# Block attention and two MLPs on one core: two groups of half-array matmuls per pair of heads, later weight sums, stores by half

## Chip, core and metric

The kernel runs on one NeuronCore of a Trainium2 chip. The metric is the time of one execution on the device in microseconds (us), and before and after are compared by the median of several runs. The core's engines are TensorE (PE, matrix products into the PSUM memory, eight banks of 512 fp32 columns), VectorE (DVE), ScalarE (ACT), GpSimd (POOL) and SyncE (SP, which here only issues DMAs). Each engine works through its own queue in order and waits on semaphores for the others.

## What is computed

Four batches of eight heads, 576 positions, head width 64, go through attention with a mask by blocks of 64; its output `x` (2304 tokens, 512 wide) goes through a gated MLP (inner width 1536) and then through an MLP with a leaky ReLU (inner width 2048):

```python
scores = scale * np.matmul(q, k.transpose(0, 1, 3, 2))
scores = np.where(block_i >= block_j, scores, -1000000000.0)
attn = np.exp(scores - np.max(scores, axis=-1, keepdims=True))
attn = attn / (np.sum(attn, axis=-1, keepdims=True) + 1e-09)
x = np.matmul(attn, v)                       # then heads side by side: 2304 x 512
x = (1 / (1 + np.exp(-(x @ w_gate))) * (x @ w_val)) @ w_out
h = x @ w_in
out = np.maximum(0.01 * h, h) @ w_out        # of the second MLP
```

## The kernel before, in words

The whole program is written as a list of operations (`Plan.op`), each with an engine (or a choice of two), a cost in us that the author wrote down, what it reads and writes, the ring buffers it uses, and a due time. `Plan.order` then puts them in one order per engine: among the operations that its own clock holds ready it takes the one with the earliest due time. Nothing of that clock is left in the program; what stays is the order on each queue. A ring (`Ring`) hands out its buffers strictly in the order in which the code asked for them, so an operation that needs buffer number n waits until number n minus the ring's size is free.

The stages are these. First the attention of batch 0 alone. Then stage 0: both MLPs of batch 0 on PE, with the attention of batch 1 in between. Stage 1: both MLPs of batch 1, with the attention of batches 2 and 3 in between. Then the MLPs of batches 2 and 3 together (`pair_unit`), in a form of matrix product that needs seven instead of eight block products and for that wants sums of weight blocks.

**Attention** (`attention`, from line 339) goes by pairs of heads, since a head is 64 wide and two heads fill 128 rows. A pair has four query tiles of 128 positions (0 to 3) and a rest of 64 positions of each head ("last"). For a set of tiles `query_tiles` asks for PSUM banks, makes the score products (`scores`, line 357, which use half of the array's rows for each head), then `softmax` on DVE (line 398: mask, minimum and copy out of PSUM), ACT (line 413: exponential), DVE (lines 423 and 426: sum plus epsilon, reciprocal) and ACT or POOL (lines 431, 433: scaling), and then transposes on PE (line 544) whose results are copied back to SBUF. The products with the values (`p_v` line 568, `last_p_v` line 505) use half of the array's columns. The products of halves are gathered by `stretch`: whatever stands in the list `later` is put in front of the next score products, so that they follow each other directly on PE. In batches 1 to 3 a pair has three such stretches: (A) the value products of the pair before, the scores of "last" and of tiles 0 and 1; (B) the value products of "last" and the scores of tile 2; (C) the scores of tile 3. Between them run the matrix products of the MLPs (line 996, 12 matmuls to a unit of 256 or 320 columns). PSUM is split into rings: `mm` three banks, `sc` two, `tp` two, `pa` one. Transposes and the products for "last" use `tp`, score tiles use `sc`.

**Weights.** Each of the 68 weight tiles arrives in a packed form, is converted once (`convert`: load into a `raw` buffer, ACT lines 682 and 685, DVE lines 686 to 693, DVE or POOL line 699, then a high part on ACT or DVE and a low part on DVE into a `w` buffer) and stored; later uses load the stored form (`w<-wd`). The last four to be converted, those of batch 0's last output group (`o`), come after the first four gates of batch 1 in the code. `sums` (line 733) adds weight blocks of two neighbouring tiles for the last stage: it takes two `wf` buffers and three `raw` buffers, and its stores are `ds<-raw`. Rings: `raw` three, `wf` three, `w` seven. In the main loop at the end `sums` is called as soon as the second half of an odd tile of batch 1 has been placed, thus twice ahead of those last four conversions.

**Outputs** are stored by SP (line 296, `out_t<-acc`) in pieces of 128 x 576 once both halves of a tile are complete; the halves are 256 and 320 columns.

Of the kernel before, what the change touches and what calls it, by code (L numbers as in the profile page):

```python
# [202 lines left out]
def block_attention_then_two_mlps(  # L203
# [74 lines left out]
    def c_dve(n):  # L278
        return 0.07 + n / 960
# [57 lines left out]
    def attention(b, start, length, alone):  # L337
# [31 lines left out]
        def stretch(parts, t):  # L369

            parts = [*(make(t) for make in later), *parts]
            later.clear()

            def f():
                for x in parts:
                    x[1]()

            reads, writes, uses = [[y for x in parts for y in x[k]] for k in (2, 3, 4)]
            op("pe", sum(x[0] for x in parts), f, reads, writes, uses, t, kind="h", slack=slack)
            for x in parts:  # L380
                for then in x[5:]:
                    then()

        def softmax(tiles, masked, t):


            nm, sm, r = r_nm.tile(), r_sm.tile(), r_r.tile()
            done, k = [], 0
            m = len(tiles)
            for i, pieces in enumerate(tiles):  # L390
                x = tiles_made[0] % NPP
                tiles_made[0] += 1
# [24 lines left out]
                op(  # L417
                    "act", c_act(n) + 0.14, f, [(nm, k - 1), *[(p_tok, j) for j in range(len(pieces))]],
                    [(sm, i), p_tok], [nm, sm, both], t + 1.3,
                )  # L420
                done.append((pt, p_tok, n))

            op("dve", 0.07, lambda: nc.vector.tensor_scalar(
                out=r[:, :m], in0=sm[:, :m], scalar1=1e-9, scalar2=None, op0=ALU.add
            ), [(sm, i) for i in range(m)], [r], [r, sm], t + 2.2)
            op("dve", 0.08, lambda: nc.vector.reciprocal(out=r[:, :m], in_=r[:, :m]), [], [r], [r], t + 2.4)  # L426
            for i, (pt, p_tok, n) in enumerate(done):

                def f(e, pt=pt, i=i, n=n):
                    if e == "act":  # L430
                        nc.scalar.activation(pt[:, :n], pt[:, :n], AF.Copy, scale=r[:, i:i + 1])  # L431
                    else:
                        nc.gpsimd.tensor_scalar(  # L433
                            out=pt[:, :n], in0=pt[:, :n], scalar1=r[:, i:i + 1], scalar2=0.0, op0=ALU.mult, op1=ALU.add
                        )

                op(("act", "pool"), (0.24 + n / 1200, 0.25 + n / 1200), f, [r], [p_tok], [r, both], t + 2.6, port=("pool",))
            return [x[:2] for x in done]

        def pair(i):  # L440
# [30 lines left out]
                return r  # L471


            beside = []

            def last_queries(t):

# [34 lines left out]
                        lambda: split(S - BLK, S, "D", t + 0.8, px, [px]),  # L512
                    )

                later.append(last_p_v)
                if alone:
                    stretch([], t + 5.2)

            def query_tiles(cs):
                t = at[cs[0]]  # L520
                ps = [bank(), bank()]
                cols = dict(zip(cs, (0, P)))
                if cs[0] == 0 and not alone:
                    beside.extend([(b_tp.tile(), 0, 4 * P), (ps[0], 3 * P, BLK)])
                scores(
                    of_last(beside if cs[0] == 0 else [])
                    + [(ps[a], cols[c], 0, a, c * P, P, 0, (c + 1) * P) for c in cs for a in range(2)], tqk, t,
                )
                done = softmax([[(ps[a], cols[c], (c + 1) * P)] for c in cs for a in range(2)], True, t)
                for c in cs:  # L530
                    transposed(c, done[2 * cs.index(c):][:2], at[c])

# [49 lines left out]
                if alone:  # L582
                    stretch([], t + 5.2)

            for cs in ([0, 1], [2], [3]):
                query_tiles(cs)
                if cs[0] == 0 and not alone:
                    last_queries(at[0])
            if alone:
                last_queries(at[NKT - 1])  # L590

        for i in range(H // 2):
            pair(i)
# [76 lines left out]
    def convert(u, wf, d):  # L670
# [27 lines left out]
        def f(e):  # L698
            engines[e].tensor_tensor(wf[:].bitcast(I32), mag[:].bitcast(I32), rnd[:], ALU.add)  # L699

        op(("dve", "pool"), (c_dve(n) + 0.03, 1.23), f, [mag, rnd], [wf], [mag, rnd, wf], d - 5, port=True)

    seen = set()

# [18 lines left out]
    def sums(u, w0, w1):  # L723
# [5 lines left out]

        def two(n, out, x, y, alu, reads, writes, uses, d):  # L730
            op(
                both_engines, (c_dve(n), 0.2 + n / 490),
                lambda e: engines[e].tensor_tensor(out(), x(), y(), alu), reads, writes, uses, d, port=True,
            )

# [90 lines left out]
    def mix_tile(first, e, half, k):  # L826
# [3 lines left out]

        def two(out, x, y, alu, reads, writes, uses, e):
            op(
                ("dve", "pool"), (c_dve(n), 0.2 + n / 490),
                lambda eng: engines[eng].tensor_tensor(out[:, hs], x(), y(), alu), reads, writes, uses, e, port=True,
            )

# [42 lines left out]
    def pair_unit(u, ws, half):  # L879
# [56 lines left out]
        def finish(name, p, x):  # L936
# [10 lines left out]
            else:  # L947
                view, gtok, ghost = gates[b, m + j]
                op(
                    ("dve", "pool"), (c_dve(n), 0.2 + n / 490),  # L950
                    lambda e: engines[e].tensor_tensor(dst(), dst(), view()[:, hs], ALU.mult),
                    [(gtok, half)], [tok], [host, ghost], e, port=True,
                )
# [21 lines left out]
    def half_unit(u, ws, half):  # L975
# [66 lines left out]
        else:  # L1042
# [7 lines left out]
            if kind == "y" and g == N1 // G - 1 and b < 2:  # L1050
                toks = x_toks(b, mo, "CD" if half else "A")
                hi_lo(n, lambda: x_of(b, mo)[:, 0, hs], lambda: x_of(b, mo)[:, 1, hs], lambda: a, toks_a, *toks, [], e + 0.6)
            if kind == "o" and g == N2 // G - 1 and half:
                store(
                    out[mo * P:(mo + 1) * P, b * S:(b + 1) * S], lambda: acc_of(b)[:, mo], P * S * 4, e + 1,
                    [*toks_of(b, mo, 0), *toks_of(b, mo, 1)], [("out", b, mo)],
                )


    attention(0, 5.0, FIRST, True)  # L1060
    held, sl = {}, []
    sums_x = None

    def g_place(t, view, i=0, more=()):
# [16 lines left out]
    for n, (u, half) in enumerate(order):  # L1081
# [31 lines left out]
            held[key] = weights(u)  # L1113
        half_unit(u, held[key], half)
        if u[1] == 1 and u[0] in ("gate", "val", "h") and u[2] % 2 and half:
            sums(u, held[u[0], 1, u[2] - 1], held[u])

    with tc.manual_schedule():
        make_identity(nc, ident)
# [53 lines left out]
```

## Time and profile before

| | |
|---|---|
| median of 3 runs (lowest to highest) | 1033.25 us (1030.99 to 1036.31) |
| the profiled execution: its time | 1031.44 us |
| its span, first to last instruction | 1029.7 us |
| PE busy | 1009.4 us, 98% of the span |
| DVE / ACT / POOL busy | 716.1 / 529.9 / 161.8 us |
| DMA | 200 MB, 194 GB/s on average |
| transposes and "last" products on PE, lines 544, 490, 505 | 400 matmuls of 128 columns and 320 of 64 |

The span is what the trace shows; the profiled execution's time is 1.74 us longer, the parts before the first and after the last recorded instruction. In the rows further down, a row of the timeline gives the start and the length of a run of like instructions in us; the end of a matmul is modelled, so the distance from the start of one row to the start of the next is the safer measure on PE. In each stretch of a window table an engine's busy time can be set against the length of the stretch. `sc<-qk ... 64x384 x4` are the scores of tile 2 for two heads; every product of plain fp32 stands in the trace as two matmuls.

### The profile page before, as it was taken

Reading aid. Unit: us, or ns where it says so; the run is one execution under the profiler, and the core shown is the slowest. Engines: PE = TensorE matmul, PEld = TensorE weight load, DVE = VectorE, ACT = ScalarE, POOL = GpSimd, SP = SyncE. Lnnn points to the kernel's source line nnn. Section 1 sums busy time; section 2 is a strip of 40 time slices with the busy share of each in tenths; the row PEclk is TensorE's granted clock in tenths of the full one; section 3 lists DMA queues with packets and bytes.
Section 4 is the critical chain, followed back from the end, with each engine's and each line's share of the span. In section 5 each row is a group of like instructions: output and inputs, shape, how many; then the busy total and the mean of one; then the engine's idle time right before and its main releaser. Section 6 shows DMA issues by size and latency. Waiting matters only on the chain.

```text
span 1029.7 us, 20204 instructions
## 1 busy us (share of the span) xinstructions
PE 1009.4 (98%) x7680; PEld 937.9 (91%) x7680; DVE 716.1 (70%) x1773; ACT 529.9 (51%) x1178; POOL 161.8 (16%) x186
## 2 busy tenths in 40 slices
PE   7999999999998999999999999999999999999998
PEld 4588998999996998889889889999999999999998
DVE  6989899999976876467656458860844887163652
ACT  7987776888748365545654543242321444231220
POOL 3321112211111413124122202100200110000000
PEclk9999999999999999999999999999999999999999
DMA  9686867688876797665765445452442435242422
GB/s 221 186 302 224 303 234 254 237 291 276 287 268 220 293 311 256 200 208 183 237 205 191 138 154 190 152 189 99 146 164 68 149 114 184 72 164 67 162 80 92
DMA packets 69985, 200.03 MB, mean 194 GB/s; under 512 B 6912, under 2 KB 16128, under 8 KB 69888
## 3 DMA queue, kind: packets, MB, share of 16 engines
q1 hardware_dynamic: 69888, 198.73, 58.4%
q8 instruction: 61, 1.00, 0.4%
q14 instruction: 36, 0.29, 0.1%
HBM read 137.36 MB, written 61.34 MB: 193 GB/s over the span
## 4 chain that ended last, share of the span: by engine, by line
PE 91%; ACT 3%; DVE 2%; DMA 2%; issue 1%; SPq 0%; POOL 0%; POOLq 0%; DVEq 0%; ACTq 0%
PE mm L996 55%; PE mm L899 6%; PE tp L899 6%; PE sc L899 6%; PE sc L357 4%; PE tp L544 3%; PE pa L899 3%; PE pa L568 2%; DMA raw<-in_w 1%; PE tp L357 1%; PE mm L568 1%; DMA w<-wd 1%; PE tp L490 1%; PE tp L505 1%; ACT both L413 1%
## 5 line engine op out<-in xcount | busy, mean ns | idle before, releaser
L996 PE MATMUL mm<-g,w 128*128 128x256 f32 (+1 forms) x1776 | 272.3, 299 | 0.9 <-DVE w L303 0.7
L996 PE MATMUL mm<-x,w 128*128 128x256 f32 (+1 forms) x1920 | 270.6, 298 | 2.2 <-DVE gf L1023 1.4
L996 PEld LDWEIGHTS mm<-x,w 128*128 128x128 f32 x1920 | 256.6, 188 | 13.2 <-issue 5.2
L996 PEld LDWEIGHTS mm<-g,w 128*128 128x128 f32 x1776 | 247.3, 190 | 10.4 <-issue 3.5
L1049 DVE TENSOR_TENSOR acc<-mm,acc 128x256 f32<-128x256 f32 (+1 forms) x160 | 72.8, 455 | 87.6 <-PE mm L996 86.9
L413 ACT ACTIVATE both<-both,nm 128x128 f32<-128x128 f32 (+3 forms) x144 | 82.9, 578 | 31.7 <-DVE nm L398 31.1
L899 PE MATMUL sc<-x,w 128*128 128x256 f32 (+1 forms) x480 | 76.3, 295 | 1.0 <-ACT v L301 1.0
L699 POOL TENSOR_TENSOR wf<-mag,rnd 128x512 int32<-128x512 int32 x34 | 46.6, 1372 | 192.9 <-DVE mag L693 130.7
L398 DVE CUSTOM_DVE_ANT_0 both<-sc,mask 128x128 f32<-128x128 f32 (+4 forms) x121 | 53.7, 483 | 27.7 <-PE sc L357 27.2
L314 DVE TENSOR_TENSOR g<-gf,g 128x576 fp32r<-128x576 f32 (+2 forms) x92 | 62.5, 685 | 13.7 <-ACT g L301 13.5
L996 PE MATMUL mm<-sg,w 128*128 128x320 f32 (+1 forms) x416 | 70.2, 294 | 0.0
L899 PEld LDWEIGHTS sc<-x,w 128*128 128x128 f32 x480 | 67.8, 188 | 1.2 <-ACT v L301 1.2
L996 PE MATMUL mm<-qk,w 128*128 128x320 f32 (+1 forms) x384 | 66.8, 296 | 0.0
L301 ACT ACTIVATE g<-gf 128x576 fp32r<-128x576 f32 (+2 forms) x75 | 44.0, 590 | 41.0 <-DVE gf L1023 18.5
L433 POOL TENSOR_SCALAR both<-both,r 128x128 f32<-128x128 f32 (+4 forms) x62 | 37.6, 616 | 162.3 <-DVE r L426 104.3
L357 PE MATMUL sc<-qk 64*128 64x128 f32 (+5 forms) x308 | 56.9, 443 | 5.5 <-DMA qk<-in_qk 5.5
L996 PEld LDWEIGHTS mm<-sg,w 128*128 128x128 f32 x416 | 60.5, 188 | 0.0
L996 PEld LDWEIGHTS mm<-qk,w 128*128 128x128 f32 x384 | 56.5, 189 | 0.0
L431 ACT ACTIVATE both<-both,r 128x512 f32<-128x512 f32 (+4 forms) x82 | 45.7, 593 | 14.1 <-DVE r L426 14.0
L544 PE MATMUL tp<-ident,both 128*128 128x128 f32 x320 | 46.6, 278 | 6.1 <-POOL both L433 3.9
L314 DVE TENSOR_TENSOR w<-wf,w 128x512 fp32r<-128x512 f32 x68 | 47.8, 703 | 3.4 <-ACT w L301 2.4
L544 PEld LDWEIGHTS tp<-ident,both 128*128 128x128 f32 x320 | 37.0, 143 | 13.7 <-POOL both L433 7.6
(172 smaller groups left out, 1627.9 us busy)
## 6 DMA issues: line engine op xcount, KB each, us to landing
w<-wd SPq DMA_DIRECT2D x116, 512.0 KB, 4.1
raw<-in_w SPq DMA_DIRECT2D x68, 512.0 KB, 4.8
wd<-w SPq DMA_DIRECT2D x68, 512.0 KB, 4.0
ds<-raw SPq DMA_DIRECT2D x40, 512.0 KB, 4.3
w<-ds SPq DMA_DIRECT2D x40, 512.0 KB, 6.1
qk<-in_qk SPq DMA_DIRECT2D x32, 288.0 KB, 6.4
v<-in_v SPq DMA_DIRECT2D x32, 160.0 KB, 4.1
w<-wd SPq DMA_DIRECT2D x20, 256.0 KB, 3.5
```

Source lines behind the costliest of these rows:

```text
L301: nc.scalar.activation(dst(), src(), AF.Copy)
L314: engines[e].tensor_tensor(dst(), a(), f32(b()), ALU.subtract)
L357: nc.tensor.matmul(ps[row:row + nq, col:col + nk], lhsT=tqk[half, 0, q0:q0 + nq], rhs=tqk[half, 1, k0:k0 + nk], start=True, stop=True,)
L398: nc.vector.tensor_tensor_reduce(out=pt[:, n:n + width], in0=ps[:, col:col + width], in1=mask[:, 4 * P + BLK - width:] if masked else mask ...
L413: nc.scalar.activation(pt[:, :n], pt[:, :n], AF.Exp, bias=nm[:, k - 1:k], scale=-1.0, accum_out=sm[:, i:i + 1],)
L431: nc.scalar.activation(pt[:, :n], pt[:, :n], AF.Copy, scale=r[:, i:i + 1])
L433: nc.gpsimd.tensor_scalar(out=pt[:, :n], in0=pt[:, :n], scalar1=r[:, i:i + 1], scalar2=0.0, op0=ALU.mult, op1=ALU.add)
L544: nc.tensor.transpose(tp[:, (j * m + k) * P:(j * m + k + 1) * P], tiles[a][0][:, j * P:(j + 1) * P], ident)
L699: engines[e].tensor_tensor(wf[:].bitcast(I32), mag[:].bitcast(I32), rnd[:], ALU.add)
L899: nc.tensor.matmul(p[:, :n], lhsT=wt[:, wl, col + k * P:col + (k + 1) * P], rhs=srcs[k][0]()[:, xl, hs], start=k == 0 and wl + xl == 0, st ...
L996: nc.tensor.matmul(ps[:, :n], lhsT=ws[:, wl, k * P:(k + 1) * P], rhs=srcs[k]()[:, xl, hs], start=k == 0 and wl + xl == 0, stop=k == 3 and ...
L1049: op("dve", c_dve(n), lambda: nc.vector.tensor_tensor(a, ps[:, :n], a, ALU.add), [ps], toks_a, [ps], e)
```

## The change

In batches 1 to 3, `query_tiles` now takes tiles 2 and 3 together: four banks, two from `sc` for tile 2 and two from `tp` for tile 3, one stretch of scores, and one softmax over four tiles. The value products of "last" wait in a list of their own (`lasts`) and join `later` only at the end of the pair, so they follow the value products of tiles 0 to 3 in the next pair's first stretch. The first batch's attention keeps its three sets. `stretch` sorts the ring buffers that it uses by number.

The two sums of the first gates of batch 1 are no longer placed at once: `to_sum` holds them until all 68 tiles have been converted (`len(seen) == NU`). Stores of the result go by half. And four cost numbers of POOL operations, which the planner uses, are raised a little.

```diff
@@ query_tiles
-                ps = [bank(), bank()]
-                cols = dict(zip(cs, (0, P)))
+                side = cs[-1] < 2
+                ps = {(cs[0], a): bank() for a in range(2)}
+                for a in range(2):
+                    ps[cs[-1], a] = ps[cs[0], a] if side or len(cs) == 1 else b_tp.tile()
+                cols = dict(zip(cs, (0, P if side else 0)))
...
-            for cs in ([0, 1], [2], [3]):
+            for cs in ([0, 1], [2], [3]) if alone else ([0, 1], [2, 3]):
                 query_tiles(cs)
                 if cs[0] == 0 and not alone:
                     last_queries(at[0])
             if alone:
                 last_queries(at[NKT - 1])
+            later.extend(lasts)
@@ last_queries
-                later.append(last_p_v)
+                lasts.append(last_p_v)
                 if alone:
+                    later.append(lasts.pop())
                     stretch([], t + 5.2)
@@ stretch
+            uses.sort(key=lambda x: x.index)
@@ softmax, convert, sums / mix / pair_unit (costs of POOL, in the planner only)
-  (0.24 + n / 1200, 0.25 + n / 1200)      +  (0.24 + n / 1200, 0.42 + n / 1500)
-  (c_dve(n) + 0.03, 1.23)                 +  (c_dve(n) + 0.03, 1.36)
-  (c_dve(n), 0.2 + n / 490)               +  (c_dve(n), 0.25 + n / 450)
@@ half_unit, stores
-            if kind == "o" and g == N2 // G - 1 and half:
+            if kind == "o" and g == N2 // G - 1:
                 store(
-                    out[mo * P:(mo + 1) * P, b * S:(b + 1) * S], lambda: acc_of(b)[:, mo], P * S * 4, e + 1,
-                    [*toks_of(b, mo, 0), *toks_of(b, mo, 1)], [("out", b, mo)],
+                    out[mo * P:(mo + 1) * P, b * S + hs.start:b * S + hs.stop], lambda: a, P * n * 4, e + 1, toks_a,
+                    [("out", b, mo, half)],
                 )
@@ main loop
-            sums(u, held[u[0], 1, u[2] - 1], held[u])
+            to_sum.append((u, held[u[0], 1, u[2] - 1], held[u]))
+        if len(seen) == NU:
+            while to_sum:
+                sums(*to_sum.pop(0))
```

The PE queue in stage 1, first pair of heads, from the last transpose of "last" on (`mm<-g` are the units of batch 0's last output group, with the last four weight tiles). Before:

```order
L490 MATMUL tp<-ident,both 64x128
L505 MATMUL tp<-last,v 64x64 x10
L357 MATMUL sc<-qk 128x384 x2
L996 MATMUL mm<-g,w 128x256 x12
L996 MATMUL mm<-g,w 128x320 x12
L357 MATMUL sc<-qk 128x512 x2
L544 MATMUL tp<-ident,both 128x128 x3
L996 MATMUL mm<-g,w 128x256 x12
L544 MATMUL tp<-ident,both 128x128 x3
```

and now:

```order
L491 MATMUL tp<-ident,both 64x128
L1003 MATMUL mm<-g,w 128x256 x12
L1003 MATMUL mm<-g,w 128x320 x12
L357 MATMUL sc<-qk 128x384 x2
L357 MATMUL tp<-qk 128x512 x2
L1003 MATMUL mm<-g,w 128x256 x12
L1003 MATMUL mm<-g,w 128x320 x12
L1003 MATMUL mm<-g,w 128x256 x12
L1003 MATMUL mm<-g,w 128x320 x12
L1003 MATMUL mm<-g,w 128x256 x12
L550 MATMUL tp<-ident,both 128x128 x6
```

The scores of tiles 2 and 3 have moved together, the "last" products have left this place, and five units of matmuls instead of none stand between the scores of tile 3 and the first transposes.

The SP queue at the same place (`wd_172` is the store of the tile converted just ahead of the last four, `wd_185` to `wd_188` are the stores of these, `ds_189` and `ds_190` those of the two sums, `wd_133` on the loads of the first `val` weights of batch 1). Before:

```order
L296 DMA wd_172<-w 128x1024
L296 DMA ds_189<-raw 128x1024 x2
L296 DMA ds_190<-raw 128x1024
L291 DMA raw<-in_w 128x1024
L296 DMA ds_190<-raw 128x1024
L291 DMA raw<-in_w 128x1024 x3
L296 DMA wd_185<-w 128x1024
L296 DMA out_t<-acc 128x576
L291 DMA qk<-in_qk 64x2x576 x2
L296 DMA wd_186<-w 128x1024
```

and now:

```order
L296 DMA wd_172<-w 128x1024
L291 DMA raw<-in_w 128x1024
L296 DMA wd_185<-w 128x1024
L296 DMA wd_186<-w 128x1024
L296 DMA wd_187<-w 128x1024
L291 DMA w<-wd_133 128x1024
L296 DMA wd_188<-w 128x1024
L291 DMA w<-wd_134 128x1024
L296 DMA ds_189<-raw 128x1024 x2
L296 DMA out_t<-acc 128x256
L296 DMA out_t<-acc 128x320
L291 DMA w<-wd_135 128x1024
```

Three of the four loads of packed weights have moved ahead of `wd_172`, and the stores of the sums stand behind the last conversion.

The PE queue at the change from the first to the second pair of heads in stage 1, the first stretch of the second pair. Before:

```order
L568 MATMUL pa<-both,v 64x512 x2
L568 MATMUL pa<-both,v 64x384 x2
L568 MATMUL pa<-both,v 64x256 x2
L568 MATMUL pa<-both,v 64x128 x2
L357 MATMUL tp<-qk 64x512 x2
```

and now:

```order
L574 MATMUL pa<-both,v 64x512 x2
L574 MATMUL pa<-both,v 64x384 x2
L574 MATMUL pa<-both,v 64x256 x2
L574 MATMUL pa<-both,v 64x128 x2
L506 MATMUL tp<-last,v 64x64 x10
L357 MATMUL tp<-qk 64x512 x2
```

The "last" products of the pair before have joined the value products.

## Rows read from the trace of the kernel before

**Rows 1.** The page, part 1: busy us (share of the span) x instructions.
```profile
PE 1009.4 (98%) x7680; PEld 937.9 (91%) x7680; DVE 716.1 (70%) x1773; ACT 529.9 (51%) x1178; POOL 161.8 (16%) x186
```

**Rows 2.** Windows: stretch, its length, busy us of each engine (x), PEclk, DMA, GB/s.
```profile
40.00:60.00 20.00, 17.51 (x162) 12.06 (x161) 19.50 (x65) 17.67 (x45) 7.43 (x8) 1.00 0.73 219
60.00:300.00 240.00, 237.82 (x1818) 220.68 (x1818) 222.39 (x530) 183.06 (x383) 42.11 (x35) 1.00 0.78 264
300.00:340.00 40.00, 35.89 (x265) 32.23 (x265) 29.17 (x70) 27.89 (x58) 6.87 (x8) 0.96 0.68 235
...
600.00:615.00 15.00, 13.99 (x103) 12.34 (x102) 6.75 (x18) 5.71 (x15) 0.00 (x0) 1.00 0.40 130
```

**Rows 3.** Timeline of PE, stage 0, one pair: start, length, what.
```profile
135.47 3.42 PE L996 MATMUL mm<-x,w 128*128 128x320 f32 x24
138.73 0.27 PE L490 MATMUL tp<-ident,both 128*64 128x128 f32 x1
138.76 3.43 PE L996 MATMUL mm<-x,w 128*128 128x320 f32 x24
142.12 0.80 PE L505 MATMUL tp<-last,v 128*64 128x64 f32 x20
142.85 0.92 PE L357 MATMUL sc<-qk 64*128 64x384 f32 x4
143.70 6.63 PE L996 MATMUL mm<-x,w 128*128 128x320 f32 x48
...
155.87 1.13 PE L357 MATMUL sc<-qk 64*128 64x512 f32 x4
156.93 3.30 PE L996 MATMUL mm<-g,w 128*128 128x256 f32 x23
```

**Rows 4.** Windows as in rows 2, start of stage 1, three stretches.
```profile
322.00:329.40 7.40, 6.35 (x55) 4.65 (x53) 6.30 (x17) 7.34 (x12) 0.00 (x0) 1.00 0.72 252
329.40:333.00 3.60, 0.58 (x4) 0.00 (x0) 3.11 (x9) 3.06 (x9) 1.86 (x2) 0.95 0.59 170
333.00:336.40 3.40, 3.36 (x16) 3.16 (x17) 3.11 (x7) 3.38 (x8) 0.00 (x0) 0.55 0.69 237
```

**Rows 5.** Timeline of that place: SP, PE, ACT, DVE and POOL, [idle before, releaser].
```profile
309.18 6.45 SPq L296 DMA_DIRECT2D ds<-raw  x3
...
318.03 6.01 SPq L291 DMA_DIRECT2D raw<-in_w  x3
...
324.98 0.51 PE L996 MATMUL mm<-g,w 128*128 128x256 f32 x2 [0.71 <-DVE w L303]
...
328.85 1.13 PE L357 MATMUL sc<-qk 64*128 64x512 f32 x4
333.04 0.90 PE L544 MATMUL tp<-ident,both 128*128 128x128 f32 x3 [3.06 <-POOL both L433]
...
323.05 1.28 ACT L1011 ACT_TABLE_LOAD   x1
...
327.90 1.28 ACT L413 ACT_TABLE_LOAD   x1
329.20 0.62 ACT L413 ACTIVATE both<-both,nm 128x384 f32<-128x384 f32 x1
...
330.54 0.98 DVE L423 TENSOR_SCALAR r<-sm 128x2 f32<-128x2 f32 x1 [0.49 <-ACT both L413]
...
332.40 0.59 POOL L433 TENSOR_SCALAR both<-both,r 128x384 f32<-128x384 f32 x1 [0.90 <-DVE r L426]
```

**Rows 6.** Timeline of DVE and ACT: masks of 384 and 512, exponential of 512.
```profile
325.57 0.55 DVE L398 CUSTOM_DVE_ANT_0 both<-sc,mask 128x384 f32<-128x384 f32 x1
...
331.44 0.68 DVE L398 CUSTOM_DVE_ANT_0 both<-sc,mask 128x512 f32<-128x512 f32 x1
...
332.16 0.72 ACT L413 ACTIVATE both<-both,nm 128x512 f32<-128x512 f32 x1 [0.55 <-DVE nm L398]
```

**Rows 7.** DMA issues from 1014 us on: KB each, median us to landing.
```profile
out_t<-acc SPq DMA_DIRECT2D x8, 288.0 KB, 2.1
```

More of the change, by code (lines that the diff above doesn't have):

```diff
@@ L435, in f @@
                         )
-                op(("act", "pool"), (0.24 + n / 1200, 0.25 + n / 1200), f, [r], [p_tok], [r, both], t + 2.6, port=("pool",))
+                op(("act", "pool"), (0.24 + n / 1200, 0.42 + n / 1500), f, [r], [p_tok], [r, both], t + 2.6, port=("pool",))
             return [x[:2] for x in done]
@@ L471, in of_last @@
                 return r
-            beside = []
+            beside, lasts = [], []
             def last_queries(t):
@@ L520, in query_tiles @@
                 t = at[cs[0]]
-                ps = [bank(), bank()]
-                cols = dict(zip(cs, (0, P)))
+                side = cs[-1] < 2
[3 more added lines that the diff above has]
+                cols = dict(zip(cs, (0, P if side else 0)))
                 if cs[0] == 0 and not alone:
-                    beside.extend([(b_tp.tile(), 0, 4 * P), (ps[0], 3 * P, BLK)])
+                    beside.extend([(b_tp.tile(), 0, 4 * P), (ps[0, 0], 3 * P, BLK)])
                 scores(
                     of_last(beside if cs[0] == 0 else [])
-                    + [(ps[a], cols[c], 0, a, c * P, P, 0, (c + 1) * P) for c in cs for a in range(2)], tqk, t,
+                    + [(ps[c, a], cols[c], 0, a, c * P, P, 0, (c + 1) * P) for c in cs for a in range(2)], tqk, t,
                 )
-                done = softmax([[(ps[a], cols[c], (c + 1) * P)] for c in cs for a in range(2)], True, t)
+                done = softmax([[(ps[c, a], cols[c], (c + 1) * P)] for c in cs for a in range(2)], True, t)
                 for c in cs:
@@ L699, in f @@
             engines[e].tensor_tensor(wf[:].bitcast(I32), mag[:].bitcast(I32), rnd[:], ALU.add)
-        op(("dve", "pool"), (c_dve(n) + 0.03, 1.23), f, [mag, rnd], [wf], [mag, rnd, wf], d - 5, port=True)
+        op(("dve", "pool"), (c_dve(n) + 0.03, 1.36), f, [mag, rnd], [wf], [mag, rnd, wf], d - 5, port=True)
     seen = set()
@@ L731, in two @@
             op(
-                both_engines, (c_dve(n), 0.2 + n / 490),
+                both_engines, (c_dve(n), 0.25 + n / 450),
                 lambda e: engines[e].tensor_tensor(out(), x(), y(), alu), reads, writes, uses, d, port=True,
@@ L832, in two @@
             op(
-                ("dve", "pool"), (c_dve(n), 0.2 + n / 490),
+                ("dve", "pool"), (c_dve(n), 0.25 + n / 450),
                 lambda eng: engines[eng].tensor_tensor(out[:, hs], x(), y(), alu), reads, writes, uses, e, port=True,
@@ L949, in finish @@
                 op(
-                    ("dve", "pool"), (c_dve(n), 0.2 + n / 490),
+                    ("dve", "pool"), (c_dve(n), 0.25 + n / 450),
                     lambda e: engines[e].tensor_tensor(dst(), dst(), view()[:, hs], ALU.mult),
@@ L1052, in half_unit @@
                 hi_lo(n, lambda: x_of(b, mo)[:, 0, hs], lambda: x_of(b, mo)[:, 1, hs], lambda: a, toks_a, *toks, [], e + 0.6)
-            if kind == "o" and g == N2 // G - 1 and half:
+            if kind == "o" and g == N2 // G - 1:
                 store(
-                    out[mo * P:(mo + 1) * P, b * S:(b + 1) * S], lambda: acc_of(b)[:, mo], P * S * 4, e + 1,
-                    [*toks_of(b, mo, 0), *toks_of(b, mo, 1)], [("out", b, mo)],
+                    out[mo * P:(mo + 1) * P, b * S + hs.start:b * S + hs.stop], lambda: a, P * n * 4, e + 1, toks_a,
+                    [("out", b, mo, half)],
                 )
     attention(0, 5.0, FIRST, True)
-    held, sl = {}, []
+    held, sl, to_sum = {}, [], []
     sums_x = None
```

## The prediction

> **What bounds the kernel now.** I read the page's busy times first: PE is busy 1009.4 of 1029.7 us [rows 1], so 20.3 us of the span are all that PE waits, and everything else lies beside it. A change can win in two ways only: PE does its work in less time, or it waits less. So I looked next where PE waits, with the window tables: set each stretch's PE time against its length. From 40 to 60 us 2.5 us are missing, from 60 to 300 us 2.2, from 300 to 340 us 4.1, from 600 to 615 us 1.0 [rows 2]; the rest lies in the first 40 us and behind the last matmul. The stretch from 300 to 340 is the odd one: it is also the only one of these with a granted clock below 1.
>
> The finer windows [rows 4] show what it is. From 322 to 329.4 us PE misses 1.05 us, from 329.4 to 333.0 it misses 3.02, and then, while it counts as busy, the clock stands at 0.55 for 3.4 us, mostly at 1.2 instead of 2.4 GHz; that costs about 3.4 x 0.45 = 1.5 us more. Together 5.6 us. The timeline [rows 5] tells the story backwards: the transposes at 333.04 waited for POOL's scaling, POOL for the sum and reciprocal on DVE, these for the exponentials on ACT, which began at 329.20 because ACT worked from 323.05 on through the sigmoids with a table load at either end; and ahead of that the matmuls at 324.98 waited for a converted weight, whose packed form was loaded only from 318.03 on. The loads wait for `raw` buffers, and the sums of the first gates had them until their stores, from 309.18 on. The order put the transposes right behind the scores of tile 3, with no other work between.
>
> The third view is one pair of heads in the PE timeline [rows 3]: it shows what a stretch of half-array products costs beyond its columns.
>
> **The change, part by part.**
>
> *One stretch fewer per pair.* I take starts, not lengths. The score stretch of tile 2 (four matmuls of 384) takes from 142.85 to 143.70, 0.85 us; that of tile 3 (four of 512) from 155.87 to 156.93, 1.06 us [rows 3]. Two run at a time, so 0.21 us is the price of two pairs x 128 columns, 0.105 for 128 columns. Then 384 columns twice are 0.63 and 512 twice 0.84, and 0.22 of either stretch is no column's: it belongs to going into and out of this division of the array. There is a second part ahead of a stretch. The 24 matmuls from 135.47 to 138.73, followed by a transpose, take 3.26 us; the same 24 from 138.76 to 142.12, followed by half-array products, take 3.36: 0.10 for the change into it. So a separate stretch costs 0.10 + 0.22 = 0.32 us. The "last" products cost 0.10 ahead as well, and their 10 pairs of 64 columns are 10 x 0.0525 = 0.53 of the 0.73 us from 142.12 to 142.85, so 0.20 is theirs. Before, B and C cost 0.10 + 0.20 + 0.22 + 0.32 = 0.84; now one stretch costs 0.32, and the "last" products stand behind value products of the same division, for nothing but their columns. That is 0.52 a pair. Part of the 0.20 is the start-up of ten short products and may stay, so I bound the gain from below by one stretch of scores alone, 0.32, and take 0.46, between the two and nearer to the upper since the "last" products lose their stretch whole. With 12 pairs: 5.5 us, bounds 3.8 and 6.2, all on PE and so all on the path.
>
> The Trainium skill's TensorEngine Tiling (Array Packing), section Key Properties, says that changing the tiling mode drains TensorE; the 0.10 and 0.22 us agree with it.
>
> *The place at 322 us.* Now three of the last four packed loads stand ahead of the sums in SP's queue, and the conversions no longer wait for the `raw` buffers; the wait at 324.98 goes. Between the joined scores and their transposes stand five units of 12 matmuls. A unit of 256 and one of 320 make the 24 of 3.26 us [rows 3], so these five are about 7.8 us of cover where there was none. I take the whole 5.6 us, bounds 0 (something of the same kind comes in its place) and 5.6. What is late next? The chain of four softmaxes: masks 0.55 and 0.68, exponentials 0.62 and 0.72 [rows 5, 6]. Exponentials are the slowest, 2 x 0.62 + 2 x 0.72 = 2.7, behind one mask (0.6), then sum and reciprocal (0.5), then two scalings (0.6 each, partly on two engines): 4.4 to 5.0 us. It starts when the first scores are out, over 1 us before the stretch ends, so against 7.8 + 1 there are 3 us to spare; in the other pairs the order gives 6.4 to 9.6 us of matmuls there, against 5 to 7 before.
>
> *What waits behind the moved sums.* Their buffers: each holds two gate tiles of the seven `w` buffers until it has run, so the `val` loads (`w<-wd_133` to `wd_136`) wait for the sums' first additions, and all that stands behind them on SP too: stores of results, the next `qk` and `v`. PE needs the first of these weights eight units (13 us) after the first `o` unit; a load of this kind lands in a few us. I cost it at nothing; if that cover is gone it is a rival below.
>
> *Softmax bookkeeping.* One group of sum and reciprocal fewer per pair, on DVE; hidden beside PE, and worth something only in stage 0, where DVE is busy 222 of 240 us [rows 2]. The raised POOL costs change only which engine is chosen. Nothing.
>
> *Stores by half.* Twice the issues on SP, beside everything. At the end only the last one counts: 288 KB land in 2.1 us [rows 7], at the end 160 KB have to. Bounds 0 and 0.9 (if it were all bytes); most of it seems fixed, I take 0.2. The Trainium skill's DMA: Bandwidth & Descriptors, section Anatomy of one DMA, gives a fixed 2.0 us plus bytes at 436 GB/s for a transfer issued from GpSimd; by it 0.3 us would be an estimate for the 128 KB saved, and no run here shows that path.
>
> *Small waits elsewhere*, 2.5 + 2.2 + 1.0 us [rows 2], come from accidents of the order. All queues are ordered anew, so I expect others of the same sum; bounds minus 4 and plus 4.
>
> **Sum.** 5.5 + 5.6 + 0.2 = 11.3 us. Against the profiled execution's 1031.44 us: 1020.1. The median of the runs shown is 1.8 above that execution and their lowest 0.5 below it; I go half of the way and say 1021.
>
> **Rivals.**
>
> *The accident moves* (or the sums' late buffers make one). The order knows the planner's clock, not the chip's; a wait of 3 us with the clock fall behind it, as in rows 4, shows up at another place, or the `val` loads come late. For it: it happened once in 12 pairs before, and all is reordered. Against: longer covers everywhere. Then 11.3 - 5.6 = 5.7 us are left, 1025.7, by the median 1027.5.
>
> *The price is not per stretch.* If the 0.22 belongs to the sizes and not to the change of division, joining brings only 0.10 a pair: 1.2 + 5.6 + 0.2 = 7 us, 1024.4. Rows 3 speak against it: two lengths give the same rest only if it is fixed.
>
> *Four banks at once drain too slowly (slower).* Both `tp` banks are held by tile 3's scores until DVE has masked them, and the transposes of tile 2 wait for all four softmaxes. In stage 0 DVE is busy 93% [rows 2]; if its queue and ACT's table loads stretch the chain from 5 us beyond the cover of 6.4 to 9.6 plus 1, PE stops as at 329 us, 3.0 plus 1.5 us each [rows 4]. In all four pairs of stage 0 that is 18 us; with 5.7 gained, 1031.4 + 12.3 = 1044. It decides for "slower" from four such stops on; with two it is a tie. The Trainium skill's TensorEngine Tiling (Array Packing), section PSUM Bottleneck, points that way: tiling speeds up TensorE but not the emptying of PSUM. Against it: the first stretch of a pair has given DVE six masks at once all along, and PE never waited for it there.
>
> *It does not do what it says*: the order shows both stretches joined and the sums moved; this is excluded.
>
> **Chances.** Forecast as summed, 1014 to 1025: 0.66. Accident moves: 0.17. Price not per stretch: 0.06. Some of both and only 1 to 5 us gained: 0.06. Slower by the banks: 0.05. The range that leaves out at most 2 in 10 reaches from 1013 (all small waits halved, upper bound of the stretches, no median shift) to 1029 (accident moved, median shift, one us more). A measurement of this kernel can tell about 0.5%, 5.2 us, from no change: faster means below 1028.1. The forecast, the price rival and most of the accident's case lie there: 0.84; same 0.11; slower 0.05.
>
> **What would show it.** PE's busy time down by 5 to 6 us at the same count of matmuls; score stretches of eight matmuls of about 1.7 us by their starts where there were 0.85 and 1.06, and the 20 "last" matmuls behind value products taking nearer 0.55 than 0.73; no clock below 1 between 300 and 340 us, and that stretch 5 to 6 us shorter; the landing of the last store at 1.8 to 2.0 us. It would be wrong if PE waits at transposes (line 550) for ACT's or POOL's scaling, at units of `val` for `w<-wd`, or if a second fall of the clock appears.

## The result

The kernel after takes 1019.9 us (median of 4 runs, 1019.46 to 1020.89) against 1032.4 us of the kernel before (median of 4 runs, 1030.99 to 1036.31). The ratio is 0.988, 95% interval 0.986 to 0.990: faster by 1.2%. Predicted were 1021.0 us, range 1013 to 1029. The profiled execution of after took 1019.83 us with a span of 1018.1 us.

The page of the kernel after, part 1, answers to [rows 1]:

```profile
PE 1002.0 (98%) x7680; PEld 937.6 (92%) x7680; DVE 709.0 (70%) x1742; ACT 528.9 (52%) x1182; POOL 169.0 (17%) x189
```

PE is busy 7.4 us less, at the same 7680 matmuls, and it waits 16.1 us (span less busy time) where it waited 20.3. So both ways in which a change can win were used.

The windows of after, with the columns and stretches of [rows 2]:

```profile
40.00:60.00 20.00, 18.11 (x158) 11.20 (x157) 19.30 (x67) 16.92 (x44) 7.18 (x8) 1.00 0.80 227
60.00:300.00 240.00, 236.59 (x1819) 222.14 (x1818) 220.95 (x520) 185.71 (x390) 38.83 (x33) 1.00 0.79 269
300.00:340.00 40.00, 39.26 (x294) 36.59 (x293) 32.64 (x75) 27.80 (x59) 12.65 (x13) 1.00 0.82 298
...
600.00:615.00 15.00, 14.82 (x112) 14.61 (x111) 14.84 (x33) 7.09 (x16) 6.35 (x7) 1.00 0.46 142
```

From 300 to 340 us PE misses 0.74 us where it missed 4.11, and the clock is whole. From 60 to 300 it misses 3.4 instead of 2.2 us, from 40 to 60 us 1.9 instead of 2.5, from 600 to 615 us 0.2 instead of 1.0.

The place of [rows 4], the middle one of the same three windows, in after:

```profile
329.40:333.00 3.60, 3.60 (x28) 3.60 (x28) 3.13 (x7) 3.09 (x10) 1.95 (x3) 1.00 0.95 330
```

PE is busy throughout, at the whole clock (2.4 GHz), and so in the windows ahead and behind. The SP queue says why. In before the first of the last four packed weights was loaded at 316.57 (timeline of SP), the others from 318.03 on [rows 5], and SP's loads waited for the stores of the sums to land (SP's waits from 300 to 326 us: us in all, times, longest):

```profile
316.57 0.33 SPq L291 DMA_DIRECT2D raw<-in_w  x1
```

```profile
SPq L291 <- DMA ds<-raw: 4.7, 2, 4.2
```

In after the last of the four is loaded at 302.68, and the stores of the sums come behind it:

```profile
302.68 0.39 SPq L291 DMA_DIRECT2D raw<-in_w  x1
...
323.92 1.88 SPq L296 DMA_DIRECT2D ds<-raw  x2
```

The timeline of PE in after at the pair of [rows 3]; the joined scores of tiles 2 and 3, then five units (60 matmuls) ahead of the transposes:

```profile
138.72 0.92 PE L357 MATMUL sc<-qk 64*128 64x384 f32 x4
139.47 1.02 PE L357 MATMUL tp<-qk 64*128 64x512 f32 x4
140.42 8.39 PE L1003 MATMUL mm<-x,w 128*128 128x320 f32 x60
148.65 0.82 PE L550 MATMUL tp<-ident,both 128*128 128x128 f32 x6
```

From start to start the joined scores take 140.42 - 138.72 = 1.70 us, where [rows 3] have 0.85 and 1.06 in two places. The "last" products, which took 0.73 us there, now stand in the next pair's first stretch (shown beside the first experiment).

PE's waits in after, without those of the first attention and one of 0.2 us at 602 us (another 5.5 us are the loads at the program's start):

```profile
PE mm L1003 <- DVE w L314: 2.6, 5, 0.7
...
PE tp L550 <- POOL both L434: 0.8, 1, 0.8
...
PE mm L1003 <- DMA w<-wd: 0.7, 1, 0.7
```

(The columns are us in all, times, longest.) The five waits for converted weights lie between 184 and 207 us, the wait for POOL's scaling at 183 us, that for a stored weight at 306 us. A wait of a transpose for POOL is one of the signs of being wrong that the prediction named; it is 0.8 us long, and no fall of the clock follows.

### The profile page after: what moved, and what is told of

The parts are those of the page before. It is cut to its first block, busy times and chain, and to the rows that moved or that the text cites. A ratio compares the mean times of both kernels' runs of the same rounds, so it can differ in the third digit from the quotient of the medians.

```text
span 1018.1 us, 20174 instructions
## 1 busy us (share of the span) xinstructions
PE 1002.0 (98%) x7680; PEld 937.6 (92%) x7680; DVE 709.0 (70%) x1742; ACT 528.9 (52%) x1182; POOL 169.0 (17%) x189
## 4 chain that ended last, share of the span: by engine, by line
PE 93%; DVE 4%; ACT 1%; DMA 1%; issue 1%; SPq 0%; DVEq 0%
PE mm L1003 58%; PE mm L906 6%; PE tp L906 6%; PE sc L906 6%; PE pa L906 3%; PE tp L550 3%; PE sc L357 3%; PE pa L574 3%; PE tp L357 2%; PE tp L491 1%; DMA w<-wd 1%; PE tp L506 1%; DVE both L399 1%; PE mm L574 1%; ACT both L414 1%
## 5 line engine op out<-in xcount | busy, mean ns | idle before, releaser
L706 POOL TENSOR_TENSOR wf<-mag,rnd 128x512 int32<-128x512 int32 x31 | 42.4, 1367 | 191.8 <-DVE mag L700 126.8
L434 POOL TENSOR_SCALAR both<-both,r 128x128 f32<-128x128 f32 (+4 forms) x52 | 32.5, 631 | 169.4 <-DVE r L427 129.9
L399 DVE CUSTOM_DVE_ANT_0 both<-sc,mask 128x128 f32<-128x128 f32 (+4 forms) x97 | 38.1, 432 | 22.8 <-PE sc L357 22.5
L432 ACT ACTIVATE both<-both,r 128x128 f32<-128x128 f32 (+4 forms) x92 | 48.8, 580 | 6.0 <-DVE r L427 6.0
L692 ACT ACTIVATE mag<-raw 128x512 f32<-128x512 f32 x68 | 45.6, 670 | 7.2 <-POOL wf L706 3.6
L953 ACT ACTIVATE gf<-gf 128x256 f32<-128x256 f32 (+1 forms) x64 | 27.2, 442 | 41.3 <-DVE gf L922 41.2
```

What stands on the lines that cost most here:

```text
L399: nc.vector.tensor_tensor_reduce(out=pt[:, n:n + width], in0=ps[:, col:col + width], in1=mask[:, 4 * P + BLK - width:] if masked else mask ...
L692: op("act", c_act(n), lambda: nc.scalar.activation(mag[:], words(1).bitcast(F32), AF.Abs), [raw], [mag], [raw, mag], d - 8)
```

## Experiments

All times are medians. "PE waits" is the span less PE's busy time of the profiled execution.

| kernel | us | ratio to before (95%) | PE busy | PE waits |
|---|---|---|---|---|
| before | 1031.5 to 1032.4 | 1 | 1009.4 | 20.3 |
| after | 1019.9 | 0.988 (0.986 to 0.990) | 1002.0 | 16.1 |
| e1 three stretches | 1026.7 | 0.996 (0.994 to 0.997) | 1008.5 | 16.3 |
| e2 sums at once | 1027.0 | 0.996 (0.994 to 0.997) | 1005.7 | 20.1 |
| e3 "last" ahead of the joined scores | 1059.3 | 1.027 (1.022 to 1.032) | 1020.8 | 30.3 |
| e4 before, sums late | 1025.7 | 0.995 (0.993 to 0.996) | 1007.7 | 16.2 |
| e5 as e3, bank of `pa` | 1023.9 | 0.993 (0.990 to 0.995) | 1004.6 | 17.2 |
| e6 whole stores | 1021.6 | 0.990 (0.988 to 0.992) | 1003.0 | 16.9 |
| e7 all old POOL numbers | 1020.5 | 0.989 (0.987 to 0.991) | 1001.5 | 17.7 |
| e8 old number, conversion | 1025.2 | 0.994 (0.992 to 0.995) | 1003.6 | 19.7 |
| e9 three stretches, sums at once | 1032.9 | 1.001 (1.000 to 1.002) | 1011.8 | 20.6 |
| e10 old number, scaling | 1022.1 | 0.991 (0.989 to 0.992) | 1001.9 | 19.9 |
| e11 old number, two operands | 1021.7 | 0.990 (0.989 to 0.992) | 1001.9 | 17.9 |
| e12 after once more | 1020.9 | 0.989 (0.987 to 0.990) | 1002.6 | 15.6 |

### Three stretches again (e1)

```diff
-                lasts.append(last_p_v)
+                later.append(last_p_v)
...
-                    later.append(lasts.pop())
...
-            for cs in ([0, 1], [2], [3]) if alone else ([0, 1], [2, 3]):
+            for cs in ([0, 1], [2], [3]):
```

> The kernel after, but with the three stretches of half-array products per pair of heads as before (scores of tile 3 apart, the value products of the rest in front of the scores of tile 2); late sums, stores by half and the planner's costs stay as in after. Price per stretch (my theory): a pair takes 0.44 us more on PE, 12 pairs 5.3 us, so 1025.2 us against 1019.9 of after, PE busy 1007 against 1002.0, and score stretches of 0.85 and 1.06 us by their starts again; no clock below 1 between 300 and 340 us. Rival, the price is not per stretch (only 0.10 a pair): 1021.1 us, PE busy 1003. Rival, the joined softmax itself removed the stop at the start of stage 1: a stop of 3 us with the half clock comes back as well, 1030 us.

Measured: 6.8 us more than after, PE busy 6.5 us more. The timeline of PE in e1 has the same pair as above:

```profile
139.12 0.80 PE L506 MATMUL tp<-last,v 128*64 128x64 f32 x20
139.85 0.92 PE L357 MATMUL sc<-qk 64*128 64x384 f32 x4
140.70 6.63 PE L1002 MATMUL mm<-x,w 128*128 128x320 f32 x48
...
152.87 1.13 PE L357 MATMUL sc<-qk 64*128 64x512 f32 x4
153.93 6.65 PE L1002 MATMUL mm<-g,w 128*128 128x256 f32 x48
```

and its first stretch of a pair:

```profile
115.99 2.37 PE L573 MATMUL pa<-both,v 128*64 128x512 f32 x16
118.29 1.08 PE L357 MATMUL tp<-qk 64*64 64x512 f32 x4
...
120.27 3.93 PE L1002 MATMUL mm<-x,w 128*128 128x256 f32 x28
```

against that of after:

```profile
115.14 2.37 PE L574 MATMUL pa<-both,v 128*64 128x512 f32 x16
117.34 0.75 PE L506 MATMUL tp<-last,v 128*64 128x64 f32 x20
118.02 1.07 PE L357 MATMUL tp<-qk 64*64 64x512 f32 x4
...
120.00 1.21 PE L1003 MATMUL mm<-x,w 128*128 128x256 f32 x8
```

By starts e1 has 120.27 - 115.99 = 4.28, 140.70 - 139.12 = 1.58 and 153.93 - 152.87 = 1.06, together 6.92 us. After has 120.00 - 115.14 = 4.86 and 1.70, together 6.56. That is 0.36 us a pair, and one entry less, for which [rows 3] have 0.10: some 0.45 us, in 12 pairs 5.4; the 12 pairs are alike (the joined scores take 1.70 or 1.71 us in each). The price is per stretch; the rival (1.2 us in all) is out. The "last" products take 118.02 - 117.34 = 0.68 us by starts in after, but 0.10 of that is the change to the scores, which e1 has directly behind the value products (118.29 - 115.99 = 2.30 us against 117.34 - 115.14 = 2.20); they add 0.58. The other 1.4 us of the 6.8 were not expected. PE's waits are only 0.2 us more than in after; 1.1 us are busy time of PE that the stretches don't explain, in a queue that is ordered anew, and what they consist of was not settled. The third case, a stop at the start of stage 1, did not come: PE is busy all of 300 to 340 us in e1.

### The sums at once, and the sums late in the kernel before (e2, e4)

e2, from after:

```diff
-            to_sum.append((u, held[u[0], 1, u[2] - 1], held[u]))
+            sums(u, held[u[0], 1, u[2] - 1], held[u])
```

> The kernel after, but with the sums of the first gates' weights placed at once, as before. In the order the joined scores then have three units of 12 matmuls (4.5 us) in front of their transposes, where after has five. Theory that the later sums removed the stop: PE waits again for converted weights in front of the joined scores (0.7 to 1 us) and for the scaling at the transposes (the chain of four softmaxes is 4.4 to 5.0 us, begun late because ACT does the sigmoids with their table loads), 3 us with a half clock of 1.5 us behind it: 1024 to 1025 us. Theory that the units behind the joined scores removed it: only the wait for weights is back, the chain is covered but for 0.5 us, no clock below 1: 1020.5 to 1021.5 us.

e4, from before, puts the `to_sum` list of the change into the main loop and nothing else:

```diff
-            sums(u, held[u[0], 1, u[2] - 1], held[u])
+            to_sum.append((u, held[u[0], 1, u[2] - 1], held[u]))
+        if len(seen) == NU:
+            while to_sum:
+                sums(*to_sum.pop(0))
```

> The kernel before with one edit: the sums of the first gates' weights wait until the last conversion. Three stretches per pair, stores and costs are those of before. In the order one unit (1.4 us) stands between the scores of tile 3 and the first transposes, and two units between the scores of tile 2 and of tile 3. If the sums' buffers were the cause of the stop at 322 to 336 us: no wait of 3 us, no clock below 1 there, 4.9 to 5.6 us less than before, 1027 us. If the missing cover behind the scores was the cause: PE still waits there for 1.5 to 3 us, with or without the half clock, 1029 to 1032 us.

Measured: e2 takes 7.1 us more than after, e4 5.8 us less than before on the same chip (1031.5). In e2 the packed loads are late again (SP queue):

```profile
317.69 0.33 SPq L291 DMA_DIRECT2D raw<-in_w  x1
...
319.06 6.45 SPq L291 DMA_DIRECT2D raw<-in_w  x3
```

and PE stops behind the joined scores (timeline of PE in e2), then runs at the half clock (one window of e2):

```profile
326.80 0.79 PE L1003 MATMUL mm<-g,w 128*128 128x256 f32 x2 [2.57 <-DVE w L303]
327.87 6.18 PE L1003 MATMUL mm<-g,w 128*128 128x256 f32 x24 [0.29 <-DVE w L314]
335.04 1.46 PE L1003 MATMUL mm<-g,w 128*128 128x256 f32 x10 [0.98 <-DVE w L314]
336.34 0.82 PE L550 MATMUL tp<-ident,both 128*128 128x128 f32 x6
```

```profile
329.40:333.00 3.60, 3.60 (x16) 3.60 (x16) 2.15 (x4) 3.59 (x10) 0.00 (x0) 0.50 0.85 268
```

The size is that of the first theory, and a little more. A part of the more is the clock: in the three windows of [rows 4] e2 has 0.83, 0.50 and 0.90, some 3.4 us lost where before lost 1.5. But the place is not that of the theory: nothing waits for scaled tiles at 336.34. What waits are the units that were to be the cover, since these are the units of the last output group, whose weights are the late ones. A cover that itself needs the late thing covers nothing.

In e4 the loads are early (SP queue) and one unit stands between the scores of tile 3 and the first transposes (timeline of PE):

```profile
302.91 0.33 SPq L291 DMA_DIRECT2D raw<-in_w  x1
```

```profile
330.50 1.13 PE L357 MATMUL sc<-qk 64*128 64x512 f32 x4
331.56 1.69 PE L996 MATMUL mm<-g,w 128*128 128x256 f32 x12
333.09 0.82 PE L544 MATMUL tp<-ident,both 128*128 128x128 f32 x6
```

No row waits. Nor was it that unit which saved the time: the scaling for these transposes ends at 330.68, before the scores of tile 3 do (timeline of POOL in e4):

```profile
330.04 0.64 POOL L433 TENSOR_SCALAR both<-both,r 128x384 f32<-128x384 f32 x1 [1.24 <-DVE r L426]
```

So the stop of [rows 5] hung on the sums ahead of the last conversions, and not on the missing cover. e4 moves all of the sums, their buffers and their work on the engines, and the order changes with them (two units now stand ahead of the scores of tile 2). That it was the `raw` buffers is read from the waits of SP's loads, shown with the result; no run tests the buffers alone.

### The "last" products ahead of the joined scores (e3, e5)

e3, from after: `later.append(last_p_v)` in place of `lasts.append(last_p_v)`. e5 is e3 with one more edit:

```diff
-                    px = (b_mm if alone else b_tp).tile()
+                    px = (b_mm if alone else b_pa).tile()
```

> The kernel after, but with the value products of the rest in front of the joined scores of the same pair, where after has them behind the value products of tiles 0 to 3 in the next pair's first stretch; still two stretches per pair. If ten short products cost only their columns wherever they stand inside a stretch (my prediction's words), nothing changes: 1019.9 us. By the rows of before and after (0.73 us when they open a stretch, 0.58 us behind value products) a pair costs 0.15 us more: 1021.7 us, PE busy 1003.8 against 1002.0. If opening a stretch with them costs all of the 0.20 that I gave them: 1022.3 us.

Measured: 1059.3 us (1053.2 to 1064.9), 27 us slower than before; none of the theories had that. The timeline of PE in e3, stage 0:

```profile
142.98 0.80 PE L506 MATMUL tp<-last,v 128*64 128x64 f32 x20
...
144.46 1.02 PE L357 MATMUL tp<-qk 64*128 64x512 f32 x2
147.17 1.12 PE L357 MATMUL tp<-qk 64*128 64x512 f32 x2 [1.70 <-DVE nm L399]
```

and of DVE, the masks of tile 3 and the copy of the "last" products:

```profile
146.42 0.69 DVE L399 CUSTOM_DVE_ANT_0 both<-tp,mask 128x512 f32<-128x512 f32 x1
...
148.33 0.69 DVE L399 CUSTOM_DVE_ANT_0 both<-tp,mask 128x512 f32<-128x512 f32 x1 [1.22 <-PE tp L357]
...
148.95 0.22 DVE L314 TENSOR_TENSOR x<-tp,x 128x64 fp32r<-128x64 f32 x1
```

Ring `tp` has two banks. The "last" products occupy one until their copy at 148.95, so the two heads' scores of tile 3 share the other, and the second head starts when DVE has masked the first (146.42 + 0.69). DVE comes to it late, since conversions and the masks of tile 2 stand ahead. In the whole trace of e3 PE waits so eight times:

```profile
PE tp L357 <- DVE nm L399: 14.2, 8, 3.3
```

and behind four of these waits, of 1.22, 1.53, 1.89 and 3.30 us, the clock falls to the half. Around the longest (windows of e3):

```profile
209.70:214.10 4.40, 1.10 (x5) 0.21 (x2) 4.32 (x12) 2.27 (x6) 0.00 (x0) 1.00 0.95 340
214.10:217.50 3.40, 3.40 (x13) 2.64 (x14) 2.17 (x6) 0.00 (x0) 0.00 (x0) 0.65 0.59 203
```

The 14.2 us of idle time are not the whole cost. By starts the eight stretches with a stop take some 24 us more than the 2.43 us each that they take in e5 (below), and the half clock, 17 us in all, costs some 8.5 us; together that is about the 33 us by which e3's span exceeds after's.

> The kernel of the run before this with the value products of the rest in front of the joined scores (1059 us), with one more edit: these products write to the bank of ring pa, not to a bank of tp. Theory that the stop there was the bank (the rest's products and the two scores of tile 3 want three banks of tp, which has two, so the second score of tile 3 waits for DVE to mask the first): the waits inside the joined scores go, and what is left is the price of opening a stretch with ten short products, 0.15 us a pair: 1021.7 us, PE busy about 1004. Theory that the place is what costs (the products in front make the joined scores late for DVE): the waits stay, over 1045 us.

Measured: 1023.9 us, and no wait inside the joined scores. It was the bank. What is left of e3's theories can be read in e5 (timeline of PE):

```profile
139.90 0.80 PE L506 MATMUL pa<-last,v 128*64 128x64 f32 x20
...
141.38 1.02 PE L357 MATMUL tp<-qk 64*128 64x512 f32 x4
142.33 7.94 PE L1002 MATMUL mm<-x,w 128*128 128x320 f32 x57
```

142.33 - 139.90 = 2.43 us, with 4.28 for the first stretch 6.71 a pair, 0.15 over after's 6.56. That splits the 0.45: 6.92 - 6.71 + 0.10 (the entry) = 0.31 for one stretch fewer, 0.15 for the "last" products behind products of the same shape of the array. The rest of e5's 4 us over after is 2.2 us, among it waits of 1.5 and 1.6 us that after doesn't have, the longer one with a fall of the clock behind it.

The Trainium skill's TensorEngine Tiling (Array Packing), section PSUM Bottleneck, says that tiling makes TensorE faster but not the emptying of PSUM. e3 agrees: the third user of two banks waits for DVE, 14.2 us in all.

### Both parts taken back (e9)

e1's and e2's edits together.

> The kernel after with three stretches per pair and the sums at once; only the stores by half, the planner's new numbers and the sorted ring buffers are left of the change. If the two parts add up and the rest is worth little: 1019.9 + 6.8 (three stretches) + 7.1 (sums at once) = 1033.8 us, and not under 1031 us. If the stores and numbers themselves carry a part of the gain: 1029 us or less. If the two parts share one cause (the stop at the start of stage 1): about 1027 us, as with either alone.

Measured: 1032.9 us, 1.001 of before (1.000 to 1.002). Joined stretches and late sums account for the whole gain, and they add up but for 1 to 2 us: 6.8 and 7.1 us singly, 13.0 together (12.0 beside e12, the kernel after in the same group of runs). Stores by half and the new numbers carry no gain by themselves.

### Whole stores (e6)

The store of 128x576 behind the second half, as in before.

> The kernel after, but with stores of 128x576 once both halves of a tile are done, as before. By my prediction the end gets 0.2 us longer (bounds 0 and 0.9), the last landing takes 2.1 us again, and nothing else changes: 1020.1 us. If stores by half had freed buffers or queues earlier, small waits appear inside: 1021 us or more.

Measured: 1021.6 us, 0.7 us more than e12, the kernel after once more. In the last 15 us of e6 288 KB land in 2.1 us, as in [rows 7]. The DMA issues of the same stretch in after (KB each, median us to landing):

```profile
out_t<-acc SPq DMA_DIRECT2D x8, 160.0 KB, 1.7
```

The landings explain 0.4 us. The other 1.3 us had arisen by 43 us, long before the first store: in the first attention, the value products that wait for a copy on DVE start at 44.58 in e6, at 43.21 in after, and at 43.77 in e12, the same kernel as after. The row of e6 on PE's timeline, then that of after:

```profile
44.58 1.68 PE L574 MATMUL mm<-both,v 128*64 128x256 f32 x10 [0.41 <-DVE both L303]
```

```profile
43.21 2.33 PE L574 MATMUL mm<-both,v 128*64 128x256 f32 x16 [0.41 <-DVE both L303]
```

The gain at the end is not steady either. From PE's last work to the end of the span it is 3.5 us in before and in e6 and 3.1 in after, but 3.5 again in e7, e8 and e10, which store by half.

### POOL's numbers in the planner (e7, e8, e10, e11, e12)

> The kernel after, but with the planner's old numbers for POOL's operations. My prediction costs the new numbers at nothing: 1019.9 us, within 2 us. Rival: the waits that after has at 182 to 206 us for converted weights (3.4 us in all, where before has 0.9) come from them: 1017.5 us. Rival: the old numbers make POOL late in places, PE waits there for scaled tiles: 1022 us or more.

> The kernel after, but with the old number for the rounding step of a weight's conversion alone (1.23 for 1.36). If that number decides the waits for converted weights at 182 to 206 us, PE waits there 1 us instead of 3.4 and the time is 1017.5 us; if the order is only reshuffled, it lies within 2 us of 1019.9.

> The kernel after with the planner's old number for POOL's scaling of softmax tiles alone. If the numbers only reshuffle the order: PE's work the same within 0.5 us, and a time between 1017 and 1025 us that follows PE's small waits. If this number is what keeps the transposes from waiting for POOL: PE waits at the transposes, over 1025 us.

> The kernel after with the planner's old number for the two-operand additions and products of weights and gates alone. If the numbers only reshuffle the order: between 1017 and 1025 us, PE's work the same within 0.5 us, the difference in its small waits. If this number keeps the additions of the last stages off the path: waits of PE behind 600 us, over 1025 us.

> The kernel after once more, beside the others of this group: 1019.9 us within 1 us. Its waits at 182 to 206 us stand at the same places; what differs between executions of one kernel is the start, where PE waits for the first loads.

Measured: after 1019.9 and 1020.9; all old numbers 1020.5; one old number each 1025.2 (conversion), 1022.1 (scaling), 1021.7 (two operands). PE's busy time is the same within 0.6 us in four of the five and 1.6 us above after in e8. e8 has a stop that none of the others has, an output unit that waits 1.3 us at 336 us for an addition into its accumulator. The rivals of e7, e10 and e11 fall, and of e8 both theories: the number doesn't remove the waits for converted weights, which every one of these kernels has between 184 and 210 us (2.3 to 2.9 us by its waits), and a reshuffle moved the time by more than the 2 us allowed. Which number is old has no plain meaning for the time; a new order does, by up to 5 us. What makes the weights late at 182 to 207 us was not settled. DVE is busy 221 of 240 us in that stage, which speaks for DVE, but no run tests it. None of these kernels is faster than after. e12 has after's waits for converted weights at the same places, each 1 us later, but not the wait for a stored weight at 306 us, which its expectation did not foresee.

## Why the prediction held, step by step

**Joined stretches**, 5.5 us (3.8 to 6.2) said, 5.4 by the rows of e1 and after. Also the split came near: 0.31 for one stretch fewer where 0.32 was said, 0.15 for the "last" products, which I had put between 0 and 0.20. The method, starts set against starts, and two lengths to take the columns out, gave a price that held in all 12 pairs. The Trainium skill's TensorEngine Tiling (Array Packing), section Key Properties, says that changing the tiling mode drains TensorE and gives no price; the 0.31 and 0.15 us agree with a drain.

**What that step missed**: it took the new list for the "last" products as a saving of some 0.1 us. e3 and e5 show that it is a condition: without it the joined scores have one bank of `tp` too few and the kernel is 27 us slower than before. That is the rival of the banks that drain too slowly, at a larger size than I gave it: 1044 us said for four stops, 1059 measured with waits in eight pairs and clock falls behind four of them. The rows on which I gave it only 0.05 were right for the change as it is, but I had not counted who else uses `tp` in that stretch.

**The place at 322 us**, 5.6 us said, 4.9 got (3.4 idle, 1.5 half clock). Right in the cause, the sums ahead of the last conversions, with one reading off: the weight for which the matmuls at 324.98 waited was loaded at 316.57 and not from 318.03 on. Wrong in one of the two reasons: for this stop the five units of cover were not needed (e4), and units that need the late weights are no cover (e2). The missing 0.7 is the wait for a stored weight at 306 us in the same window, one of the kind that I had named for the queue behind the moved sums, only ahead of them; e12, the same kernel, doesn't have it.

**The chain of four softmaxes** was taken too short, and there the cover counts. At the pair of that place in after the joined scores end at 327.25, and the scaling begins 4.9 us later (timeline of ACT in after):

```profile
332.16 1.85 ACT L432 ACTIVATE both<-both,r 128x384 f32<-128x384 f32 x3 [0.51 <-DVE r L427]
```

From the first mask at 326.49 to the first scaled tile at 332.8 it is 6.3 us where 4.4 to 5.0 were said, since ACT has sigmoids with their table loads until 328.93. In the 12 pairs the transposes start 0.5 to 3.1 us behind the tile that they wait for, where I had counted 3 us to spare. So the joined scores need units behind them, and the slower case was nearer than my account of it. (The five units are 8.0 us by my own rows, not 7.8; nothing hangs on that.)

**Moved sums, bookkeeping, POOL's numbers**: nothing said. e9 bears it out for the sum of what is left of the change; for the numbers singly e8 shows 5 us, and e10 and e11 about 1 us beside e12, all for the worse, so "nothing" holds for the four together and not for each.

**Stores by half**, 0.2 us said, 0.4 by the landings (2.1 to 1.7), which fell below the 1.8 to 2.0 that I had named; by e7, e8 and e10 this gain is not a steady one.

**Small waits elsewhere**, the same sum within 4 us said: 0.6 less, 1.2 more and 0.8 less in the three windows.

**The sum.** 5.4 + 4.9 + 0.4 + 0.2 = 10.9 us of the 11.6 by which the span fell. Of the other 0.7, 0.4 us are waits in the first 40 us (PE misses 7.0 us there in before, 6.6 in after), where executions of one kernel differ by as much (43.21 and 43.77 in after and e12); the rest is not assigned. The half of the median shift that I added was not needed: before gave 1031.5 to 1032.4 in four groups of runs, near its profiled 1031.44. **A sign misjudged**: PE's busy time fell by 7.4 and not by 5 to 6, since the half clock in [rows 4] counted as busy; I had put those 1.5 us into the place and forgotten them in the sign.

## To carry to other kernels

Where matmuls of different divisions of the array alternate, count the changes and price one by starts of rows of two lengths, then check how many PSUM banks the joined group holds with everything that stands in it. A stop is cured where its chain begins, here at the sums, an early, unhurried step that held three buffers; cover behind the stop is worth nothing if it waits for the same thing. And where a planner orders the queues, compare variants only to within what a reshuffle alone does, here up to 5 us of 1020 from one number of 0.13 us.

## Not expected of the hardware

Later than the first attention, the granted clock fell to 1.2 GHz after every stop of about 3 us here: after 3.06 us in before (0.55 in the window behind it [rows 4, 5]), 2.57 us in e2 (0.50), 2.69 us in e9 (0.50) and 3.30 us in e3 (0.65). In before that cost about half as much again as the stop, 1.5 us; in e2 it cost some 3.4 us, more than the stop. Shorter stops are less plain (a window of e3, behind the wait of 1.70 us, and one of e4):

```profile
147.20:150.60 3.40, 3.40 (x19) 2.64 (x20) 2.27 (x8) 2.26 (x7) 0.00 (x0) 1.00 0.63 219
```

```profile
52.00:56.00 4.00, 3.65 (x21) 2.97 (x23) 3.94 (x11) 2.94 (x6) 0.00 (x0) 0.71 1.03 335
```

In e3 the clock stayed whole behind 1.70 us, and behind 1.95 us at 278 us, but it fell behind 1.22 us at 81 us. In e4 it fell to 0.71 behind a wait of 1.5 us for ACT in the first attention, where the same wait in before left it whole [rows 2]. What decides between the two is left open.
